# Re-tiling v with six SBUF-to-SBUF transfers per group of heads instead of a round trip through DRAM

## The chip, the cores and the metric

The kernel runs on one core of one Trainium2 chip. The metric is the device time of one execution in microseconds (us), as the median of several runs. A profile is one execution taken by the hardware profiler; its times are counted from the first instruction, and its span ends with the last one.

## What is computed

```python
# q, k, v: (4, 8, 768, 64); sort_net: (4, 8, 8, 8); w_in: (512, 2048); w_out: (2048, 512)
for _ in range(5):
    P = exp(P - max(P)); P = P / (sum(P, -1) + 1e-09); P = P / (sum(P, -2) + 1e-09)
k_sorted = einsum('bhij,bhjcd->bhicd', P, k_b)      # 8 blocks of 96 rows are mixed by P
v_sorted = einsum('bhij,bhjcd->bhicd', P, v_b)
attn = softmax(scale * q_b @ k_sb^T)                # within each block of 96 rows
x = (attn @ v_sb), heads side by side: (3072, 512)
out = relu(x @ w_in)**2 @ w_out
```

An attention in blocks of 96 rows, whose k and v blocks are first mixed by a small matrix, is followed by a feed-forward layer over 3072 rows. All matrix products are made in bf16.

## The kernel before

The work has two streams. The feed-forward stream (`ffn_unit`) takes the 3072 rows in eight units of 384 rows, two to a batch. Each unit makes 64 "hp" matmuls (line 997: x times w_in, 16 tiles of 4), a ReLU on ScalarE and a square on VectorE per tile (lines 1005, 1008), and 48 "op" matmuls (line 1027: times w_out; line 1055 for the last tile), whose results ScalarE copies to `ob` and SyncE sends out. The attention stream works by batch and by pairs of heads (hp 0 to 3); its stages are named by letters. For batches 1 to 3 they are:

- V and N (`s_nat`, line 769): v or k of a group of four heads is mixed by `w_t` on TensorE and cast from PSUM into `vn` or `kn` by ScalarE and VectorE (helper lines 248, 250). A group has two head pairs and uses both PSUM slots of the attention stream (`p2_0`, `p2_1`).
- Z (`s_turn`): two DMA transposes on SyncE, `kx<-kn` (line 824) and `qz<-qi` (line 851), and the copy `kvT<-kx` on VectorE (line 829).
- S (`s_sc`, line 684): the scores, and the exponentials `et` on ScalarE (line 713).
- A (`s_av`, line 875): `et` times the re-tiled v `vblk`, then the reciprocal and the product `ao` on VectorE (lines 885, 886).
- X (`s_xt`, line 910): the DMA transpose `xT<-ao` that feeds the feed-forward units.

Between V and A the v of a group must change its layout: in `vn` a partition holds rows of all eight blocks, in `vblk` a partition is one of the 96 rows of a block. Before, SyncE issues a write `v_way<-vn` to DRAM (line 793, 396 KB), waits for its landing, and issues a read `vblk<-v_way` (line 799). There are two `vn` and three `vblk` buffers, handed out in turn.

The order on every engine is the work of a planner (`Plan.run`) while the program is built. TensorE has two queues of operations, attention and feed-forward. The attention queue is sorted by the due times in `DUES`, one number for each stage and head pair, counted in feed-forward pieces; the planner takes the head of the attention queue when its due time has come and its inputs are ready by the planner's own costs, and else the next feed-forward piece. The other engines take whatever is ready first by those costs. "SP" is SyncE's queue; "WAY" is the time a transfer spends on its way. The chip then runs each engine's list strictly in order, and waits by semaphore.

Of the kernel before, what the change touches and what calls it, by code (L numbers as in the profile page):

```python
# [9 lines left out]
BF16 = mybir.dt.bfloat16  # L10
# [8 lines left out]


DUES = {
    (0, "K"): (-265.0, -237.0, -495.0, -419.0),
    (0, "S"): (-232.5, -234.0, -349.0, -310.0),
    (0, "T"): (-184.0, -236.0, -400.0, -291.5),
    (0, "A"): (-135.0, -150.0, -300.0, -111.0),
    (0, "X"): (-58.0, -109.0, -251.5, -80.5),
    (0, "W"): (-267.0,),
    (1, "V"): (-117.0, -62.5),
    (1, "Q"): (-58.5,),
    (1, "N"): (None, -31.0),  # L30
    (1, "Z"): (None, None, 2.5, 48.5),
    (1, "S"): (-45.5, -5.0, 5.0, 50.0),
    (1, "A"): (-27.0, -4.5, 31.5, 51.5),
    (1, "X"): (40.0, 23.5, 37.0, 53.5),
    (2, "L"): (40.0,),
    (2, "N"): (75.5, 79.0),
    (2, "V"): (60.5, 82.5),
    (2, "Z"): (81.0, 82.5, 94.0, 83.5),
    (2, "S"): (86.0, 86.5, 96.0, 93.5),
    (2, "A"): (86.0, 88.0, 99.0, 94.5),  # L40
    (2, "X"): (97.5, 103.0, 103.0, 102.0),
    (3, "L"): (109.0,),
    (3, "N"): (111.5, 130.0),
    (3, "V"): (112.5, 144.0),
    (3, "Z"): (128.5, 139.0, 153.0, 149.0),
    (3, "S"): (144.0, 153.0, 158.0, 153.5),
    (3, "A"): (145.0, 153.5, 159.5, 154.5),
    (3, "X"): (150.5, 170.0, 236.5, 211.5),
}


# [133 lines left out]
def kernel(  # L185
# [10 lines left out]
    nc = tc.nc  # L196

    B, H, S, D = q.shape
    NB = sort_net.shape[-1]
    BLK = S // NB  # L200
    NH = B * H
    NA = S // 128
    C0 = 128 // NB
    HP = H // 2
# [25 lines left out]
    plan = Plan()  # L230
    rvn, rvb = Ring(2), Ring(3)
# [5 lines left out]
    def cost_f(n):  # L237
        return (0.17 + 0.82e-3 * n, 0.15 + 1.04e-3 * n)
# [7 lines left out]
    def copy(eng, out, in_):  # L246
        if eng == "ACT":
            nc.scalar.copy(out=out, in_=in_)  # L248
        else:
            nc.vector.tensor_copy(out=out, in_=in_)  # L250
# [41 lines left out]
    vn_r, vb_r = [], []  # L292
# [3 lines left out]
        vn_r.append(vn)  # L296
    for n in range(3):
        vb_r.append(const.tile([96, NB, HP, 66], BF16, name=f"vblk{n}"))
    v_way = nc.dram_tensor("v_way", (B, 2, NA, 128, HP * 66), BF16, kind="Internal").ap()

    kn_r = [const.tile([128, NA, 2, D], BF16, name=f"kn{n}") for n in range(4)]
    qi_r = [const.tile([128, NA, 2, D], BF16, name=f"qi{n}") for n in range(4)]
# [150 lines left out]
    for it in range(5):  # L453
        step = plan.add("ACT", 0.26, lambda e: nc.scalar.activation(
            out=p_sb, in_=p_sb, func=AF.Exp), [step])
# [297 lines left out]
    def s_nat(b, g, t, due):  # L753

        if t == 2:
            m, oldm = rvn.take()
        evs = []
        for hp in (2 * g, 2 * g + 1):
            slot, old = r2.take()
            if t == 1:  # L760
                m, oldm = rkn.take()

            def mm(e, hp=hp, slot=slot):
                src = qkv[b][t].rearrange("p (g h) x -> p g (h x)", h=HP)
                w = w_t[:, HP // 2 * b + g, :, :].rearrange("p c i -> p (c i)")
                for h in range(2):
                    r = slice(32 * (2 * (hp % 2) + h), 32 * (2 * (hp % 2) + h + 1))
                    for c in range(4):
                        nc.tensor.matmul(  # L769
                            out=p2[slot][32 * c:32 * (c + 1), h, 0:NA * D],  # L770
                            lhsT=w[r, :],
                            rhs=src[r, g, NA * D * c:NA * D * (c + 1)],
                            start=True, stop=True, tile_position=(r.start, 32 * c))

            def ev(e, hp=hp, slot=slot, m=m):
                dst = (vn_r[m][:, :, 2 * (hp % 2):2 * (hp % 2) + 2, 0:D] if t == 2
                       else kn_r[m])
                copy(e, dst, p2[slot][:, :, 0:NA * D].rearrange("p e (a d) -> p a e d", d=D))

            pe = plan.add("PE", 0.15, mm, [landed[b, t, HP * g, 0], built["t"]] + old, due,  # L780
                          mode="tile")
            readers[b].append(pe)
            op = plan.add(AD, cost_f(2 * NA * D), ev, [pe] + oldm)
            r2.use(slot, pe, op)
            evs.append(op)
            if t == 1:
                rkn.use(m, op)
                k_nat[b, hp] = m, op
        if t == 1:
            return  # L790

        def write(e):
            nc.sync.dma_start(out=v_way[b, g].rearrange("a p x -> p a x"),
                              in_=vn_r[m].rearrange("p a h x -> p a (h x)"))

        w, oldw = rvb.take()

        def read(e):
            nc.sync.dma_start(
                out=vb_r[w].rearrange("p i h x -> p (i h x)"),  # L800
                in_=v_way[b, g].rearrange("a (c i) x -> (a c) (i x)", i=NB))

        wr = plan.add("SP", 0.5, write, evs + ([loaded(b)] if b > 1 else []))
        there = plan.add("WAY", 9.7 if b == 1 and g == 0 else 3.2, lambda e: None, [wr], tail=0.8)
        rd = plan.add("SP", 0.5, read, [there] + oldw)
        back = plan.add("WAY", 3.5, lambda e: None, [rd], tail=0.7)
        rvn.use(m, *evs, there)
        rvb.use(w, back)
        v_blk[b, g] = w, back

    def loaded(b):
        return landed[b, 0, HP, 0]
# [258 lines left out]
    for k in range(2):  # L1071
# [3 lines left out]
        if k == 0:  # L1075
# [3 lines left out]
            out=pt[:, NQ * k:NQ * (k + 1), :], in_=tiles["pt_ps", NQ * k]), [pes[k]]))  # L1079
# [7 lines left out]
    for name in FIRST.split():  # L1087
# [21 lines left out]
        else:  # L1109
# [8 lines left out]
              "A": lambda b, hp, due: s_av(units[b, hp], due),  # L1118
              "X": lambda b, hp, due: s_xt(units[b, hp], due),
              "V": lambda b, g, due: s_nat(b, g, 2, due),  # L1120
              "N": lambda b, g, due: s_nat(b, g, 1, due)}

    def sort_first(b, hp, due):
# [81 lines left out]
```

## Time and profile before

| what | us |
|---|---|
| time, median of 3 runs | 218.34 (217.59 to 218.5) |
| span of the profiled execution | 216.2 |
| TensorE matmul busy | 209.8 (97% of the span) |
| VectorE, ScalarE, GpSimd busy | 109.2, 122.1, 28.3 |
| mean granted TensorE clock | 1.000 |

No time of the profiled execution is given beside its span; the median of the runs lies 2.1 us above that span, which is start and end outside of the first and last instruction. "PE" is TensorE, "DVE" VectorE, "ACT" ScalarE, "POOL" GpSimd, "SPq" SyncE's queue, whose rows are DMA issues and not transfers. Matmuls are pipelined, so a row of the timeline that holds a group of them ends about 0.16 us after the next group has begun. Some matmul records are missing: a group of 12 can be shown as x11.

### The profile page before, as it was taken

The numbers are of one execution on the slowest core, as the hardware profiler recorded it, in microseconds if no ns is written. First come the engines' busy times: TensorE is split into PE (matmuls) and PEld (weight loads), VectorE is DVE, ScalarE is ACT, GpSimd is POOL, SyncE is SP. The second block draws the span as 40 slices with busy tenths as digits, with TensorE's granted clock in tenths as the row PEclk, the third lists the DMA queues.
The fourth block names the chain that finished last, engine by engine and source line by source line (L and its number), as shares of the span: only waits on it lengthen the run. The fifth ranks groups of instructions, "written<-read, shape, count | busy, mean of one in ns | idle before, by whom it ended". The sixth has DMA issues, their size and how long they took to land.

```text
span 216.2 us, 5062 instructions
## 1 busy us (share of the span) xinstructions
PE 209.8 (97%) x2020; PEld 115.9 (54%) x2036; DVE 109.2 (51%) x297; ACT 122.1 (56%) x251; POOL 28.3 (13%) x53
## 2 busy tenths in 40 slices
PE   8998999999999999999999999999999999999994
PEld 2566675446654565445655455445655465455542
DVE  5777677146795446345875047407775154015300
ACT  4876985248765277347774178318874375137421
POOL 7896230000000700000000420000000000000000
PEclk9999999999999999999999999999999999999999
DMA  6999999999978599199995699497978410120012
GB/s 152 212 203 207 207 207 209 193 226 272 176 164 113 84 238 211 25 192 210 179 186 125 105 201 213 87 207 171 170 204 111 102 47 3 49 97 0 0 52 97
DMA packets 47864, 31.92 MB, mean 148 GB/s; under 512 B 27296, under 2 KB 42912, under 8 KB 47840
## 3 DMA queue, kind: packets, MB, share of 16 engines
q1 hardware_dynamic: 35616, 18.35, 40.1%
q0 software_dynamic: 12224, 13.24, 36.9%
q8 instruction: 16, 0.26, 0.5%
q14 instruction: 8, 0.07, 0.1%
HBM read 29.70 MB, written 8.72 MB: 178 GB/s over the span
## 4 chain that ended last, share of the span: by engine, by line
PE 93%; DVE 2%; ACT 2%; issue 1%; DVEq 0%
PE hp L997 37%; PE op L1027 36%; PE p L875 4%; PE p L440 4%; PE p L684 3%; PE p L769 2%; PE op L1055 2%; PE qtp L563 2%; DVE ao L886 1%; PE vbp L733 1%; PE p L649 1%; DVE h L1008 1%; ACT h L1005 1%; PE xtp L928 1%; PE hp L955 0%
## 5 line engine op out<-in xcount | busy, mean ns | idle before, releaser
L997 PE MATMUL hp<-xT,w_in_bf 128*128 128x384 bf16 x506 | 87.6, 326 | 0.0
L1027 PE MATMUL op<-w_out_bf,h 128*128 128x512 bf16 x352 | 83.3, 379 | 0.9 <-issue 0.2
L1008 DVE TENSOR_TENSOR h<-h 128x384 bf16<-128x384 bf16 x128 | 43.9, 355 | 56.2 <-ACT h L1005 55.7
L1005 ACT ACTIVATE h<-hp 128x384 bf16<-128x384 f32 x128 | 61.7, 495 | 17.7 <-PE hp L997 14.9
L997 PEld LDWEIGHTS <-w_in_bf 128*128 128x128 bf16 x506 | 47.7, 98 | 32.2 <-issue 1.1
L1027 PEld LDWEIGHTS <-h 128*128 128x128 bf16 x368 | 33.9, 98 | 37.9 <-issue 1.0
L248 ACT COPY ob<-op 128x512 f32<-128x512 f32 (+2 forms) x25 | 14.2, 568 | 49.1 <-PE op L1027 46.6
L713 ACT ACTIVATE et<-p 96x384 bf16<-96x384 f32 x48 | 19.9, 488 | 6.4 <-PE p L684 6.4
L886 DVE TENSOR_TENSOR ao<-p,rec 96x512 bf16<-96x512 f32 x32 | 22.0, 686 | 1.1
L875 PEld LDWEIGHTS <-et 96*128 96x128 bf16 x256 | 11.2, 97 | 5.5 <-issue 0.7
L885 DVE RECIPROCAL rec<-p 96x8 f32<-96x8 f32 x32 | 6.4, 201 | 11.1 <-PE p L875 10.5
L1144 POOL COPY held<-xT 1x3 bf16<-1x3 bf16 (+1 forms) x2 | 0.4, 183 | 85.0 <-DMA xT<-ao 85.0
L440 PE MATMUL p<-ones 128*128 128x512 bf16 (+1 forms) x28 | 9.2, 460 | 1.1 <-DVE ones L274 1.1
L875 PE MATMUL p<-vblk,et 96*128 96x65 bf16 x192 | 9.4, 193 | 0.1
L250 DVE CAST vn<-p 128x768 bf16<-128x768 f32 x6 | 5.7, 958 | 7.3 <-PE p L769 7.2
L250 DVE CAST kn<-p 128x768 bf16<-128x768 f32 x5 | 4.8, 958 | 9.1 <-PE p L769 9.1
L684 PEld LDWEIGHTS <-kvT 64*128 64x128 bf16 x256 | 6.2, 94 | 5.5 <-issue 3.6
L829 DVE COPY kvT<-kx 128x768 bf16<-128x768 bf16 x10 | 8.5, 850 | 0.0
L248 ACT CAST vn<-p 128x768 bf16<-128x768 f32 x6 | 4.8, 798 | 5.8 <-PE p L769 5.8
L324 POOL DMA_DIRECT2D kb<-in_k_dram x10 | 6.5, 648 | 4.1 <-DMA w_in_bf<-in_moe_w_in_dram 2.0
L248 ACT CAST kn<-p 128x768 bf16<-128x768 f32 x5 | 4.0, 806 | 4.7 <-PE p L769 4.7
L324 POOL DMA_DIRECT2D vb<-in_v_dram x10 | 6.3, 633 | 2.3 <-DMA w_in_bf<-in_moe_w_in_dram 2.1
(81 smaller groups left out, 118.8 us busy)
## 6 DMA issues: line engine op xcount, KB each, us to landing
out_dram<-ob SPq DMA_DIRECT2D x23, 256.0 KB, 3.4
v_way<-vn SPq DMA_DIRECT2D x6, 396.0 KB, 5.1
vblk<-v_way SPq DMA_DIRECT2D x6, 396.0 KB, 4.3
vb<-in_v_dram POOLq DMA_DIRECT2D x6, 384.0 KB, 11.7
kb<-in_k_dram POOLq DMA_DIRECT2D x6, 384.0 KB, 10.4
qb<-in_q_dram POOLq DMA_DIRECT2D x6, 384.0 KB, 13.1
w_in_bf<-in_moe_w_in_dram POOLq DMA_DIRECT2D x4, 512.0 KB, 10.4
w_out_bf<-in_moe_w_out_dram POOLq DMA_DIRECT2D x4, 512.0 KB, 15.7
```

What stands on the lines that cost most here:

```text
L248: nc.scalar.copy(out=out, in_=in_)
L250: nc.vector.tensor_copy(out=out, in_=in_)
L324: nc.gpsimd.dma_start(out=dst, in_=src)
L440: nc.tensor.matmul(out=p2[slot][:, 0, 0:128 * r].rearrange("p (r x) -> p r x", r=r), lhsT=ones, rhs=ones[:, None, :].to_broadcast([128, r, ...
L684: nc.tensor.matmul(out=scp[:, h, BLK * n:BLK * (n + 1)], lhsT=u.ksT[64 * h:64 * (h + 1), HS * hf + BLK * n:HS * hf + BLK * n + 128], rhs=( ...
L713: nc.scalar.activation(out=et[:, h, 0:HS].rearrange("p (n c a) -> p n c a", c=C0, a=NA), in_=st["p"][0:96, h, 0:HS].rearrange("p (n a c) - ...
L875: nc.tensor.matmul(out=oup[:, h, 66 * n:66 * n + D + 1], lhsT=et_r[u.et[hf]][:, h, BLK * n:BLK * n + 128], rhs=(u.vs[:, NQ * hf + n, h, 0: ...
L886: nc.vector.tensor_tensor(out=u.ao[:, n0:n0 + NQ, :, :].rearrange("p n e d -> p e n d"), in0=ov[:, :, :, 0:D], in1=rec[:, :, :, None].to_b ...
L997: nc.tensor.matmul(out=t["hp", nt][:, 0:HS], lhsT=w_in_bf[:, kc, 128 * nt:128 * (nt + 1)], rhs=xT[:, kc, t0:t0 + HS], start=(kc == 0), sto ...
L1005: nc.scalar.activation(out=t["h1", nt], in_=t["hp", nt][:, 0:HS], func=AF.Relu)
L1008: nc.vector.tensor_tensor(out=t["h2"][:, nt, :], in0=t["h1", nt], in1=t["h1", nt], op=ALU.mult)
L1027: nc.tensor.matmul(out=t["op", mt], lhsT=t["h2"][:, nt, 128 * mt:128 * (mt + 1)], rhs=w_out_bf[:, nt, :], start=(nt == 0), stop=(nt == NT ...
```

## The change

It does two things. `s_nat` no longer writes v of a group to `v_way` and reads it back. It issues six DMAs on SyncE, one for each sixth `a` of the 96 rows: each takes the 128 partitions of `vn[:, a]` (264 bf16 elements each) and lays them into 16 partitions of `vblk`, eight blocks side by side. The six are a chain in the planner (each counts as ready after the one before), at a planned 0.4 us each; after the last the planner counts 9.7 and 6.5 us on the way for batch 1 and 2.4 us for batches 2 and 3. The `vn` buffer is held until the moves have landed, and the `vblk` buffer must be free before the first move. The second thing: all due times are set anew.

```diff
-    (2, "N"): (75.5, 79.0),
-    (2, "V"): (60.5, 82.5),
+    (2, "N"): (58.0, 58.0),
+    (2, "V"): (78.5, 62.5),
...
-    v_way = nc.dram_tensor("v_way", (B, 2, NA, 128, HP * 66), BF16, kind="Internal").ap()
...
-        def write(e):
-            nc.sync.dma_start(out=v_way[b, g].rearrange("a p x -> p a x"),
-                              in_=vn_r[m].rearrange("p a h x -> p a (h x)"))
+        def move(e, a):
+            nc.sync.dma_start(out=vb_r[w][C0 * a:C0 * (a + 1)].rearrange("c i h x -> c i (h x)"),
+                              in_=vn_r[m][:, a].rearrange("p h x -> p (h x)"))
 
         w, oldw = rvb.take()
-
-        def read(e):
-            nc.sync.dma_start(
-                out=vb_r[w].rearrange("p i h x -> p (i h x)"),
-                in_=v_way[b, g].rearrange("a (c i) x -> (a c) (i x)", i=NB))
-
-        wr = plan.add("SP", 0.5, write, evs + ([loaded(b)] if b > 1 else []))
-        there = plan.add("WAY", 9.7 if b == 1 and g == 0 else 3.2, lambda e: None, [wr], tail=0.8)
-        rd = plan.add("SP", 0.5, read, [there] + oldw)
-        back = plan.add("WAY", 3.5, lambda e: None, [rd], tail=0.7)
-        rvn.use(m, *evs, there)
+        ops = evs + ([loaded(b)] if b > 1 else []) + oldw
+        for a in range(NA):
+            mv = plan.add("SP", 0.4, lambda e, a=a: move(e, a), ops)
+            ops = [mv]
+        back = plan.add("WAY", (9.7, 6.5)[g] if b == 1 else 2.4, lambda e: None, [mv], tail=1.4)
+        rvn.use(m, *evs, back)
         rvb.use(w, back)
         v_blk[b, g] = w, back
```

The new order shows best on SyncE. For batch 2, before, its list from the first output of the unit on reads as follows (`qz2` belongs to the first head pair, `qz0`, `qz1`, `qz2` to the next three; the names after "waits" are semaphores, of which DMAHW0 to DMAHW7 tell of landed DMAs).

```order
L976 DMA out_0_dram<-ob_1743 128x512 [waits DMAHW7_49,Activation_49]
L793 DMA v_way<-vn0_104 128x6x264 [waits DMAHW0_49,DVE_49]
L824 DMA_TRANSPOSE kx2_121<-kn2_113 128x6x128 [waits DMAHW1_49]
L851 DMA_TRANSPOSE qz2_102<-qi2_117 128x6x128 [waits DMAHW2_49,DVE_49,PE_49]
L824 DMA_TRANSPOSE kx0_119<-kn3_114 128x6x128 [waits DMAHW3_49,DVE_49]
L799 DMA vblk2_110<-v_way 96x2112 [waits DMAHW4_49,DMAHW0_49]
L793 DMA v_way<-vn1_106 128x6x264 [waits DMAHW5_49,DVE_49,Activation_49]
L851 DMA_TRANSPOSE qz0_92<-qi3_118 128x6x128 [waits DMAHW6_49]
L824 DMA_TRANSPOSE kx1_120<-kn1_112 128x6x128 [waits DMAHW7_49]
```

The same place now, from the first move on; the six moves of the two groups are shuffled into each other.

```order
L792 DMA vblk2_110<-vn0_104 16x8x264 [waits DMAHW0_49,DVE_49,Activation_49]
L818 DMA_TRANSPOSE kx2_121<-kn2_113 128x6x128 [waits DMAHW1_49]
L792 DMA vblk2_110<-vn0_104 16x8x264 [waits DMAHW2_49]
L792 DMA vblk0_108<-vn1_106 16x8x264 [waits DMAHW3_49,DVE_49,Activation_49]
L792 DMA vblk2_110<-vn0_104 16x8x264 [waits DMAHW4_49]
L792 DMA vblk0_108<-vn1_106 16x8x264 [waits DMAHW5_49]
L792 DMA vblk2_110<-vn0_104 16x8x264 [waits DMAHW6_49]
L792 DMA vblk0_108<-vn1_106 16x8x264 [waits DMAHW7_49]
L792 DMA vblk2_110<-vn0_104 16x8x264 [waits DMAHW0_49]
L792 DMA vblk0_108<-vn1_106 16x8x264 [waits DMAHW1_49]
L792 DMA vblk2_110<-vn0_104 16x8x264 [waits DMAHW2_49]
L792 DMA vblk0_108<-vn1_106 16x8x264 [waits DMAHW3_49]
```

Behind these twelve rows stand `qz2<-qi2`, the last move, and the six transposes of the other three head pairs. The query transpose of the first head pair, second behind the write before, now stands behind eleven moves and one transpose. Each DMA waits on the semaphore of the eighth DMA ahead of it, which the names DMAHW0 to DMAHW7 in turn show.

For batch 3 the list of SyncE now begins so, behind two outputs (before, behind one). `qz0` is of the first head pair, `qz1` of the second.

```order
L970 DMA out_0_dram<-ob_2397 128x512 [waits DMAHW5_49,Activation_49]
L970 DMA out_0_dram<-ob_2435 128x512 [waits DMAHW6_49,Activation_49]
L792 DMA vblk1_109<-vn0_104 16x8x264 [waits DMAHW7_49,DVE_49]
L818 DMA_TRANSPOSE kx0_119<-kn2_113 128x6x128 [waits DMAHW0_49]
L792 DMA vblk1_109<-vn0_104 16x8x264 [waits DMAHW1_49]
L845 DMA_TRANSPOSE qz0_92<-qi2_117 128x6x128 [waits DMAHW2_49,DVE_49]
L792 DMA vblk1_109<-vn0_104 16x8x264 [waits DMAHW3_49]
L818 DMA_TRANSPOSE kx1_120<-kn3_114 128x6x128 [waits DMAHW4_49,DVE_49]
L792 DMA vblk1_109<-vn0_104 16x8x264 [waits DMAHW5_49]
L792 DMA vblk2_110<-vn1_106 16x8x264 [waits DMAHW6_49,DVE_49,Activation_49]
L792 DMA vblk1_109<-vn0_104 16x8x264 [waits DMAHW7_49]
L792 DMA vblk2_110<-vn1_106 16x8x264 [waits DMAHW0_49]
```

The moves of the first group now alternate with the transposes of the first two head pairs; before, one write stood ahead of them. On TensorE the same matmuls stand in another order: its list is the same up to the second piece of the first feed-forward unit, and again from the last attention group of batch 3 to the end.

More of the change, by code (lines that the diff above doesn't have):

```diff
@@ L21 @@
 DUES = {
[L22 to L35, printed above, removed]
-    (2, "N"): (75.5, 79.0),
-    (2, "V"): (60.5, 82.5),
[L38 to L48, printed above, removed]
+    (0, "K"): (-252.5, -268.0, -363.0, -361.5),
+    (0, "S"): (-224.5, -216.5, -336.0, -308.0),
+    (0, "T"): (-192.5, -234.0, -358.0, -287.0),
+    (0, "A"): (-157.5, -200.0, -286.0, -129.5),
+    (0, "X"): (-68.5, -134.0, -285.0, -106.0),
+    (0, "W"): (-275.0,),
+    (1, "V"): (-131.0, -82.5),
+    (1, "Q"): (-69.0,),
+    (1, "N"): (None, -40.5),
+    (1, "Z"): (None, None, -15.5, 9.5),
+    (1, "S"): (-44.5, -23.0, -14.0, 49.0),
+    (1, "A"): (-35.5, -16.5, 9.5, 51.0),
+    (1, "X"): (-32.5, 50.5, 40.5, 55.5),
+    (2, "L"): (56.0,),
+    (2, "N"): (58.0, 58.0),
+    (2, "V"): (78.5, 62.5),
+    (2, "Z"): (80.0, 81.0, 93.0, 85.5),
+    (2, "S"): (81.5, 87.5, 94.5, 93.5),
+    (2, "A"): (85.5, 91.0, 103.0, 95.0),
+    (2, "X"): (98.0, 94.0, 106.0, 98.5),
+    (3, "L"): (110.5,),
+    (3, "N"): (135.0, 139.5),
+    (3, "V"): (127.5, 140.5),
+    (3, "Z"): (137.5, 144.5, 156.5, 145.5),
+    (3, "S"): (143.0, 149.0, 161.0, 152.0),
+    (3, "A"): (149.0, 157.5, 161.0, 153.0),
+    (3, "X"): (155.5, 187.5, 266.5, 203.0),
 }
```

## Prediction

> **What bounds the kernel now.** I read the page's first part, then the waits of TensorE, then the timelines of TensorE and of SyncE's queue in batches 2 and 3.
>
> ```profile
> span 216.2 us, 5062 instructions
> PE 209.8 (97%) x2020; PEld 115.9 (54%) x2036; DVE 109.2 (51%) x297; ACT 122.1 (56%) x251; POOL 28.3 (13%) x53
> ```
>
> TensorE's share of 97% alone would not say that it works at its pace, since overlapping matmuls count as busy. The waits of TensorE do:
>
> ```profile
> PE p L440 <- DVE ones L274: 1.1, 1, 1.1
> PE p L875 <- ACT qz L248: 0.5, 1, 0.5
> PE p L684 <- DVE ao L886: 0.3, 1, 0.3
> PE op L1027 <- issue: 0.2, 1, 0.2
> ```
>
> The first three lie in the first 20 us, where the order of the work is not changed; the fourth stands beside a missing record (the row at 93.33 below has 11 of 12 matmuls). No wait for `vblk` or `v_way` is among them. So the round trip through DRAM is hidden entirely, and removing it frees nothing by itself.
>
> How close is TensorE to its own pace? The undisturbed units at the end give the pace:
>
> ```profile
> 171.28 10.56 PE L997 MATMUL hp<-xT,w_in_bf 128*128 128x384 bf16 x64
> 181.68 10.52 PE L1027 MATMUL op<-w_out_bf,h 128*128 128x512 bf16 x47
> 192.04 10.56 PE L997 MATMUL hp<-xT,w_in_bf 128*128 128x384 bf16 x64
> ```
>
> From start to start, 64 hp matmuls take 10.40 us (0.1625 each), and 48 op matmuls, one unrecorded, 10.36 us (0.216 each). I laid every group of the program end to end at the pace that its kind has in the timeline (a switch into or out of the S groups costs about 0.1 us, and counts). From 20 us to the last matmul group the timeline is 0.96 us longer than this sum. **That 0.96 us is all that a better order can win.**
>
> **The change part by part.** *TensorE's work.* The matmuls are the same. I counted the groups in both orders: the S groups are entered from another line 22 times before and 22 times after, the V and N groups 11 and 11 times. Since only such switches cost extra, the end-to-end sum is the same: 0.
>
> *DRAM traffic.* Six writes and six reads of 396 KB go; six times six moves come that carry what the writes carried. Less load on the DMA queues: a gain only where one is late, and by the waits none is: 0.
>
> *SyncE's queue.* Here the change adds: 36 issues for 12. For batch 2 before:
>
> ```profile
> 91.34 0.39 SPq L793 DMA_DIRECT2D v_way<-vn  x1
> 91.78 1.69 SPq L824 DMA_TRANSPOSE kx<-kn  x1
> 93.57 1.31 SPq L851 DMA_TRANSPOSE qz<-qi  x1
> 94.97 2.12 SPq L824 DMA_TRANSPOSE kx<-kn  x1
> 97.19 0.53 SPq L799 DMA_DIRECT2D vblk<-v_way  x1
> 97.82 0.37 SPq L793 DMA_DIRECT2D v_way<-vn  x1
> 98.25 1.94 SPq L851 DMA_TRANSPOSE qz<-qi  x1
> ...
> 104.70 1.24 SPq L851 DMA_TRANSPOSE qz<-qi  x1
> 106.04 0.52 SPq L799 DMA_DIRECT2D vblk<-v_way  x1
> ```
>
> The queue issues without a pause from 91.34 on: it is the busiest place that the change touches. A write occupies it 0.37 to 0.39 us and the next follows 0.05 later; a read takes 0.53 and 0.10. A move is not in the trace: I bound it by these, 0.42 to 0.60, and take 0.45, since its source side is the write's. A transpose costs 1.24 to 2.12; I take 1.32 with its gap, the undisturbed value. How long they are then on the way, the DMA view gives as medians:
>
> ```profile
> v_way<-vn SPq DMA_DIRECT2D x6, 396.0 KB, 5.1
> kx<-kn SPq DMA_TRANSPOSE x10, 3.9
> qz<-qi SPq DMA_TRANSPOSE x10, 3.6
> out_dram<-ob SPq DMA_DIRECT2D x1, 64.0 KB, 1.6
> DMA to landing us min/median/max: 2.8/4.0/6.1
> ```
>
> (The last line is the view of `qz` in batch 2.) A move of 66 KB lands between 1.6 and 5.1 us after its issue; I take 2.5, nearer to the output of its size.
>
> *Batch 2.* TensorE's rows around the first S, and a cast and a copy of the same stretch:
>
> ```profile
> 93.33 2.54 PE L1027 MATMUL op<-w_out_bf,h 128*128 128x512 bf16 x11 [0.16 <-issue]
> 95.80 0.38 PE L769 MATMUL p<-vb,w_t 32*32 32x384 bf16 x16
> 96.11 1.90 PE L1027 MATMUL op<-w_out_bf,h 128*128 128x512 bf16 x8
> 97.84 1.46 PE L997 MATMUL hp<-xT,w_in_bf 128*128 128x384 bf16 x8
> 99.24 0.51 PE L684 MATMUL p<-qz,kvT 64*128 64x96 bf16 x16
> 103.08 0.66 PE L875 MATMUL p<-vblk,et 96*128 96x65 bf16 x16
> 96.32 0.96 DVE L250 CAST vn<-p 128x768 bf16<-128x768 f32 x1 [1.78 <-PE p L769]
> 98.05 0.59 ACT L248 COPY ob<-op 128x512 f32<-128x512 f32 x1 [1.02 <-PE op L1027]
> ```
>
> In the new order 28 hp matmuls of that unit stand ahead of the first S, not 8: 20 x 0.1625 = 3.25 us later; one S group of batch 1 that is no longer cut in two gives back 0.24. So S comes due at 99.24 + 3.01 = 102.25. Its query: ahead of the first V group now stand 20 op matmuls and one group (0.4) fewer than ahead of the V at 95.80, so it starts at 95.80 - 4.32 - 0.4 - 0.24 = 90.8. Its cast on VectorE ends 1.48 after the start (95.80 to 97.28 in the rows), so the first move goes at 92.35. Then one move, one transpose and ten more moves: 92.35 + 0.45 + 1.32 + 4.5 = 98.6 for the issue of `qz2`, and with 3.6 on the way it lands at 102.2. **It comes just in time, where before, issued at 93.57 and with 4.0 on the way, it was 1.7 us ahead of need.** With 0.42 a move and 2.8 on the way it is 1.1 early; with 0.60 and 6.1, 4.1 late. Since the ends are not alike, I charge 0.3. The next: the last move of the second group goes at 98.6 + 1.32 = 99.95 and lands at 102.5; A needs it at 103.08 + 0.92 = 104.0. The last query stands behind one more move and five transposes: issued at 99.95 + 0.45 + 6.6 = 107.0, landed at 110.6; its S, by the end-to-end sum, is due at 112.1. So the first wait decides, and those behind it have more room.
>
> *Batch 3.* Before, the first S:
>
> ```profile
> 139.66 0.38 SPq L793 DMA_DIRECT2D v_way<-vn  x1
> 142.19 1.22 SPq L851 DMA_TRANSPOSE qz<-qi  x1
> 150.16 0.51 PE L684 MATMUL p<-qz,kvT 64*128 64x96 bf16 x16
> ```
>
> Now two outputs stand ahead of the first move. The second belongs to an op tile that ends, by the end-to-end sum, at about 141.6; its copy takes 0.59 and the issue 0.4, so the first move goes at 142.6 and not at 139.66: the queue stands behind a copy of ScalarE for 2.9 us. `qz0` follows two moves and a transpose: 142.6 + 0.9 + 1.32 = 144.8, landed at 148.4. S has 8 hp matmuls fewer ahead of it, and the 0.24 from batch 1: due at 150.16 - 1.30 - 0.24 = 148.6. The second query is issued seven moves and two transposes (`qz0` itself and `kx1`) later: 144.8 + 2.64 + 3.15 = 150.6, landed at 154.2, due by the same sum at 154.35; the third at 157.7 against 158.0. Three that come 0.15 to 0.3 ahead of need, where before the first query had five microseconds. A wait at one shifts those behind it, so they don't add. I charge 0.3, with 0 and 2.5 as ends.
>
> *Batch 1.* The first write, its way to landing (the longest of the view of `v_way`), and the first A:
>
> ```profile
> 43.30 0.37 SPq L793 DMA_DIRECT2D v_way<-vn  x1
> DMA to landing us min/median/max: 3.8/4.3/10.0
> 59.26 0.66 PE L875 MATMUL p<-vblk,et 96*128 96x65 bf16 x16
> ```
>
> The write landed at 53.3, behind the loads of the batch. The moves share their queue with two outputs, as the write did; I let the last of the first group land by 55. A is due 12 hp matmuls earlier than at 59.26, at 57.3. Cost 0, cover 2.3 us.
>
> *V and N closer together.* Two V or N groups that share both PSUM slots now follow each other at 1.28 us twice; the casts free the second slot at 1.48 (above). About 0.1 us each: 0.2.
>
> *What goes.* In batch 2 the second read, issued at 106.04, landed 6.2 later, at 112.3, just as A began:
>
> ```profile
> DMA to landing us min/median/max: 6.2/6.2/6.2
> 112.43 0.41 PE L875 MATMUL p<-vblk,et 96*128 96x65 bf16 x8
> ```
>
> Such places the new order does not have. Of the 0.96 us I let 0.4 go (0 to 0.96).
>
> Sum: 0.3 + 0.3 + 0.2 − 0.4 = +0.4. On the span of 216.2 that gives 216.6, and with the 2.1 us between the profile's span and the median of the runs, **218.7 us**.
>
> **Rivals.** *The queue becomes the bound (slower).* If a move costs SyncE 0.60 like a read, and a transpose behind them 2.12 like the one at 94.97, the query of batch 2 is issued at 92.35 + 0.6 + 2.12 + 6 = 101.1 and lands at 104.7: 2.4 us late. For batch 3, nine moves stand ahead of the second query: 9 x 0.15 + 0.8 = 2.15 later than above, 2.0 late. 218.34 + 2.4 + 2.0 − 0.2 (the other terms) = 222.5. It decides from about 0.55 us a move. For it: the queue has no pause as it is, and each DMA waits for the eighth ahead of it, so landings over 3.6 us slow the issues. Against: the rows of 0.37.
>
> *The moves themselves are slow (slower).* A write of 128 partitions lands 3.8 us after its issue when nothing is ahead of it, the 64 KB output 1.6:
>
> ```profile
> DMA to landing us min/median/max: 3.8/3.8/3.8
> ```
>
> So 396 KB take 2.2 us of transfer, 0.37 for a sixth. If a move into 16 partitions takes twice that, 0.75, eleven moves fall 11 x 0.3 = 3.3 us behind their issue, and S of batch 2 waits 3.2 us; in batch 3 the transposes between give time, about 0.5. Time 218.34 + 3.7 = 222.0. The Trainium skill, "SBUF — State Buffer", section "Door 1: The DMA port swizzle", speaks against the change here: partitions 0 to 15 reach 4 of 16 ports, measured there at 104 GB/s. By that, an estimate from the page, a move takes 0.65 us, and the time would be about 221. No row of this trace has such a transfer, so I can't say that it agrees; moves that follow each other go to other partitions, which may hide it.
>
> *The waits vanish (faster).* If the moves land early, all of the 0.96 us may go and nothing come: 217.4 at best. For it: the DRAM reads are gone from the queue. Against: the new order ties S to its query more closely.
>
> *The change does not do what it says:* the order shows the moves and no `v_way`, so no chance is given to that.
>
> **How the numbers follow.** My forecast, waits of a few tenths in place of others, 217.8 to 219.4: 0.66. Queue-bound: 0.16. Slow moves: 0.09. Faster: 0.09. A measurement of this kernel can tell about 0.5%, 1.1 us. Under 217.25 lies little, since the floor forbids more: 0.04, by scatter of the runs. Over 219.4 lie the two slower cases and a little of the forecast's end: 0.26. Same: 0.70. The range leaves out 0.1 at each side: from 217.4, the floor, to 220.9, which takes in the milder half of the slower cases.
>
> **What would show it.** Right: PE waits after 20 us stay under 1.5 us in all; moves issue at 0.4 to 0.5 us; the first S of batches 2 and 3 starts within 0.5 us of 102.3 and 148.7. The forecast is wrong if SPq rows of moves are over 0.55 us, if `qz` lands more than 4.5 us after its issue in batch 2, or if PE waits for `qz`, `kvT` or `vblk` for over a microsecond. It would be wrong on the other side if the span falls under 215.1.

## The result and the profile after

| kernel | us, median (range) | ratio to before, 95% interval |
|---|---|---|
| before | 218.34 (217.59 to 218.53) | |
| changed | 225.15 (224.89 to 226.19) | 1.034 (1.032 to 1.036) |
| changed, measured again later on another occasion (e13) | 223.50 (222.71 to 223.99) | 1.026 (1.024 to 1.028) |

The changed kernel is 5.6 to 6.8 us slower, outside the range that was forecast. The profiled execution is one of 224.89 us with a span of 223.1 us and a mean granted clock of 0.992, where before had 216.2 and 1.000. (Single runs of e2, e3 and e9, and of before beside e13 and e14, were over 1.5% longer than the fastest of their kernel; the ratios leave them out.)

The waits of TensorE in the changed kernel, largest first (total, times, longest):

```profile
PE p L683 <- DMA qz<-qi: 4.6, 2, 2.4
PE p L439 <- DVE ones L274: 1.1, 1, 1.1
PE p L869 <- ACT qz L248: 0.5, 1, 0.5
PE p L683 <- DVE ao L880: 0.3, 1, 0.3
```

The last three were there before. The first line is new: two S groups wait for their query transposes. In the chain that ended last, SyncE's queue now has a share, and the moves' line has most of it:

```profile
PE 86%; SPq 6%; DMA 3%; DVE 1%; ACT 1%; issue 1%; ACTq 0%
```

SyncE's queue in batch 2 (start, time that the issues take, line, operation, how many):

```profile
91.03 0.33 SPq L970 DMA_DIRECT2D out_dram<-ob  x1
92.72 0.58 SPq L792 DMA_DIRECT2D vblk<-vn  x1
93.35 2.38 SPq L818 DMA_TRANSPOSE kx<-kn  x1
95.77 6.38 SPq L792 DMA_DIRECT2D vblk<-vn  x10
102.20 1.31 SPq L845 DMA_TRANSPOSE qz<-qi  x1
...
146.58 0.33 SPq L970 DMA_DIRECT2D out_dram<-ob  x1
147.00 0.59 SPq L792 DMA_DIRECT2D vblk<-vn  x1
...
152.93 3.81 SPq L792 DMA_DIRECT2D vblk<-vn  x6
156.78 1.29 SPq L845 DMA_TRANSPOSE qz<-qi  x1
```

(The last four rows are from the same view in batch 3.) Ten moves hold the queue from 95.77 to 102.20, 0.64 us each with the gap. In the DMA view the moves' way to landing is short, and the transposes land sooner than before, when the medians were 3.9 and 3.6:

```profile
vblk<-vn SPq DMA_DIRECT2D x36, 66.0 KB, 2.7
kx<-kn SPq DMA_TRANSPOSE x10, 2.8
qz<-qi SPq DMA_TRANSPOSE x10, 2.8
```

So the transfers are quick and the issues are slow. TensorE at the same place:

```profile
98.18 4.71 PE L991 MATMUL hp<-xT,w_in_bf 128*128 128x384 bf16 x28
105.08 0.52 PE L683 MATMUL p<-qz,kvT 64*128 64x96 bf16 x16 [2.19 <-DMA qz<-qi]
105.53 2.49 PE L991 MATMUL hp<-xT,w_in_bf 128*128 128x384 bf16 x8
120.72 7.07 PE L1021 MATMUL op<-w_out_bf,h 128*128 128x512 bf16 x32
161.29 0.52 PE L683 MATMUL p<-qz,kvT 64*128 64x96 bf16 x16 [2.37 <-DMA qz<-qi]
```

From start to start the 28 hp matmuls would hand over at 98.18 + 28 x 0.1625 = 102.7; S starts at 105.08, 2.35 us later (the view counts 2.19 of it as idle, since the last matmul's row ends 0.16 after the hand-over). The second S of batch 3, at 161.29, comes 2.53 us late by the same count. The row behind the first S is the second surprise: eight hp matmuls in 2.49 us, 0.31 each, where the row above has 0.168. The granted clock by stretches of 3.41 us (busy us of TensorE and its count; the number behind POOL's is the clock):

```profile
102.42:105.83 3.41, 1.22 (x21) 0.76 (x20) 0.81 (x3) 1.21 (x3) 0.00 (x0) 1.00 0.59 125
105.83:109.24 3.41, 3.41 (x20) 1.83 (x18) 1.48 (x3) 2.13 (x6) 0.00 (x0) 0.50 0.78 151
109.24:112.66 3.42, 3.42 (x47) 2.04 (x46) 2.85 (x8) 2.37 (x7) 0.00 (x0) 1.00 0.77 149
```

The stretch that holds the wait is followed by one of 3.41 us at half clock. The second wait, in batch 3 (up to 161.29), had no such sequel here.

### The profile page after: what moved, and what is told of

Its sections match the earlier page's. It is cut to its first block, busy times and chain, and to the rows that moved or that the text cites. A ratio compares the mean times of both kernels' runs of the same rounds, so it can differ in the third digit from the quotient of the medians.

```text
span 223.1 us, 5107 instructions
## 1 busy us (share of the span) xinstructions
PE 213.4 (96%) x2036; PEld 116.9 (52%) x2036; DVE 109.9 (49%) x297; ACT 123.0 (55%) x251; POOL 28.4 (13%) x53
## 4 chain that ended last, share of the span: by engine, by line
PE 86%; SPq 6%; DMA 3%; DVE 1%; ACT 1%; issue 1%; ACTq 0%
PE op L1021 34%; PE hp L991 33%; SPq L792 5%; PE p L439 4%; PE p L869 4%; PE p L683 3%; DMA qz<-qi 3%; PE p L768 2%; PE op L1049 2%; PE qtp L562 1%; SPq L818 1%; PE vbp L732 1%; PE p L648 1%; PE xtp L922 1%; PE hp L949 0%
## 5 line engine op out<-in xcount | busy, mean ns | idle before, releaser
L991 PE MATMUL hp<-xT,w_in_bf 128*128 128x384 bf16 x506 | 89.4, 330 | 0.0
L1021 PE MATMUL op<-w_out_bf,h 128*128 128x512 bf16 x368 | 85.0, 379 | 0.0
L1002 DVE TENSOR_TENSOR h<-h 128x384 bf16<-128x384 bf16 x128 | 44.4, 356 | 51.9 <-ACT h L999 51.6
L869 PEld LDWEIGHTS <-et 96*128 96x128 bf16 x256 | 11.7, 99 | 5.5 <-issue 1.3
L683 PE MATMUL p<-qz,kvT 64*128 64x96 bf16 x160 | 5.8, 204 | 4.6 <-DMA qz<-qi 4.6
```

What stands on the lines that cost most here:

```text
L683: nc.tensor.matmul(out=scp[:, h, BLK * n:BLK * (n + 1)], lhsT=u.ksT[64 * h:64 * (h + 1), HS * hf + BLK * n:HS * hf + BLK * n + 128], rhs=( ...
L869: nc.tensor.matmul(out=oup[:, h, 66 * n:66 * n + D + 1], lhsT=et_r[u.et[hf]][:, h, BLK * n:BLK * n + 128], rhs=(u.vs[:, NQ * hf + n, h, 0: ...
L991: nc.tensor.matmul(out=t["hp", nt][:, 0:HS], lhsT=w_in_bf[:, kc, 128 * nt:128 * (nt + 1)], rhs=xT[:, kc, t0:t0 + HS], start=(kc == 0), sto ...
L1002: nc.vector.tensor_tensor(out=t["h2"][:, nt, :], in0=t["h1", nt], in1=t["h1", nt], op=ALU.mult)
L1021: nc.tensor.matmul(out=t["op", mt], lhsT=t["h2"][:, nt, 128 * mt:128 * (mt + 1)], rhs=w_out_bf[:, nt, :], start=(nt == 0), stop=(nt == NT ...
```

## The experiments

The theory after the result: SyncE needs 0.64 us for each move, moves stand ahead of the queries, so S waits; the rest of the loss is the lower clock. Rivals: the new due times lose by themselves; the moves' bytes are the load; the planner's wrong cost is the fault; the clock costs little.

**e1: due times of before, moves on SyncE.** `DUES` of before in the changed kernel.

> The six moves stay on SyncE, the due times are those of before. Theory (SyncE is overbooked just ahead of the first query in batch 2 and the second in batch 3, 0.64 us a move): in this order only two moves stand ahead of the first query of batch 2, so no wait of TensorE over 0.7 us there or in batch 3, no loss of clock, 218 to 219.5 us. Rival A (moves into 16 partitions are slow on their way, wherever they stand): TensorE waits for vblk, 222 or more. Rival B (the new order of TensorE costs by itself): 218.3.

Measured 220.12 us (219.73 to 220.53), ratio 1.011 (1.009 to 1.012). That is above both the theory's range and rival B. TensorE waits for a query once, 0.9 us up to 110.85: this query was issued at 106.02, behind eleven of the batch's moves, and took 4.7 us to land. A wait of 0.4 us for `xT` is new too; where the rest of the 2 us goes is not located. The planner made an order of its own here (on TensorE it differs from the one of before from about 60 us on), so the run doesn't isolate the moves.

**e2: new due times, round trip through DRAM.** `DUES` of the changed kernel in the kernel before.

> The round trip through DRAM as before, with the new due times; the planner makes its own order from them. Theory (the due times were set for a plan with moves at 0.4 us, and fit no other): the last A of batch 3 stands right ahead of the first hp matmul that needs its xT, 3 to 4.5 us of wait there and 1 to 2 us at the same place of batch 2; no wait for a query; 222 to 225 us. Rival A (the moves are the whole loss): 218 to 219. Rival B (the new due times are the whole loss): 225.

Measured 229.46 us (227.94 to 231.43), ratio 1.050 (1.045 to 1.055): worse than every expectation, and the worst of the four combinations. TensorE's waits there are of another kind:

```profile
PE hp L997 <- DMA xT<-ao: 5.8, 3, 2.9
```

The first feed-forward matmuls of later units wait for their input: with V as late as these due times put it and two trips of 3.2 and 3.5 us in the plan, A and X presumably come too late. That the due times are no good with the DRAM trip doesn't say that they are bad with the moves.

**e3: the same plan, the moves issued by GpSimd.** `nc.sync` becomes `nc.gpsimd` in `move`; TensorE's order is untouched.

> The changed kernel with one word altered: the moves are issued by GpSimd, while the planner still books them on SyncE, so the list of TensorE is the same to the row. Theory: SyncE holds only the transposes, the query of batch 2 lands before 99, the waits of 2.35 and 2.5 us and the lost clock are gone: 217.7 to 219.3 us. Rival A (moves into 16 partitions are slow themselves): A waits for vblk, 222 or more. Rival B (the new order of TensorE costs by itself): 225.

Measured 221.50 to 228.81 us in four runs, ratio 1.023 (1.016 to 1.029), above the theory's range. As the theory had it, no S waits for a query; instead A waits for v:

```profile
PE p L869 <- DMA vblk<-vn: 3.4, 1, 3.4
```

The view of `vblk` in batch 2 of this run has the reason:

```profile
DMA to landing us min/median/max: 4.8/6.2/7.2
```

A move issued by GpSimd takes it 0.53 us, but lands 4.8 to 7.2 us later, where SyncE's land after 2.5 to 3.0. The wait has only moved.

**e4: the planner told the truth.** `plan.add("SP", 0.4, ...)` becomes `0.64`.

> The changed kernel with the planner's cost of a move at the measured 0.64 us in place of 0.4; due times as in the change. Theory: the planner now puts the first S of batch 2 at 107 and fills the time with feed-forward work, so the wait for that query goes; but the attention ends later than the feed-forward work can cover, and the first hp matmul of batch 3 waits 4 to 5.5 us for xT: 221 to 224.5 us. Rival B (the order of TensorE by itself): no statement. If the planner's cost alone were at fault: 218.5.

Measured 227.61 us (226.55 to 228.23), ratio 1.044 (1.041 to 1.048): slower still, and 3 us above the expected range. No S waits for a query any more, but the first hp matmuls of the next units wait:

```profile
PE hp L991 <- DMA xT<-ao: 5.1, 3, 3.2
```

The planner now puts S, A and X later, and the two feed-forward units of a batch are used up before the next batch's `xT` is there. So a wrong cost in the plan is not the fault; with these due times, moves at their real price do not fit either way.

**e5: half of the moves left out.**

```diff
         def move(e, a):
+            if b > 1 and a % 2:
+                return
```

> The changed kernel with every second move of batches 2 and 3 left out (three of six per group; the other halves of vblk keep old values, so the result is not computed), the order of TensorE unchanged. Theory (the moves' 0.64 us each on SyncE's queue make the queries late): in batch 2 five of eleven moves ahead of the first query go, 3.2 us, so the query lands at about 101.9, before 102.57 when S is due; the wait of 2.35 us goes, and with it the half-clock stretch of 3.41 us, worth 1.7. In batch 3 four or five of nine go, 2.6 to 3.2 us, and the wait of 2.53 goes. Time 225.15 - 2.35 - 1.7 - 2.5 = 218.6 (218.0 to 219.8), mean clock 0.998 or more. Rival (the new order of TensorE itself loses, whatever SyncE does): over 222, waits of qz at the same two places.

Measured 218.57 us (218.05 to 219.05), ratio 1.002 (1.000 to 1.004), clock 0.999 to 1.000 in all ten runs. Both waits are gone. In SyncE's queue five moves are left where ten stood:

```profile
93.50 2.49 SPq L822 DMA_TRANSPOSE kx<-kn  x1
96.09 3.11 SPq L796 DMA_DIRECT2D vblk<-vn  x5
99.25 1.29 SPq L849 DMA_TRANSPOSE qz<-qi  x1
```

The query is issued 2.95 us earlier, and all but 0.4 us of the loss is gone. This is the run that decides against the due times as the cause: the groups of matmuls stand on TensorE in the order of the changed kernel, and that order costs 0.4 us (0.9 at most, by the interval). TensorE's rows at the places shown above:

```profile
98.24 4.71 PE L995 MATMUL hp<-xT,w_in_bf 128*128 128x384 bf16 x28
102.89 0.52 PE L683 MATMUL p<-qz,kvT 64*128 64x96 bf16 x16
116.87 7.07 PE L1025 MATMUL op<-w_out_bf,h 128*128 128x512 bf16 x32
155.01 0.52 PE L683 MATMUL p<-qz,kvT 64*128 64x96 bf16 x16
```

Set against them, the changed kernel loses 2.25 us from the hp matmuls of 98.18 to the first S, 1.66 from there to the 32 op matmuls, where the half clock lies, and 2.43 from there to the second S of batch 3. That is 6.3 of the 6.4 us by which its span is longer (223.1 against 216.7).

**e7: moves in batch 1 alone.** Due times of before; batches 2 and 3 keep the round trip.

> Due times of before; moves on SyncE in batch 1 only, the round trip through DRAM in batches 2 and 3. Theory (a move costs only where SyncE's queue is full, and in batch 1 it is not): 217.6 to 218.9, no wait of TensorE over 0.5 us after 20 us. Rival (moves cost wherever they are, or the planner's other order costs): 219.3 to 220.5, as with moves in all batches.

Measured 217.94 us (217.48 to 218.75), ratio 0.999 (0.996 to 1.001). Twelve moves where SyncE has room cost nothing, and win nothing.

**e8: what an issue costs.** Twelve DMAs of six forms near the end, when SyncE is idle.

> The changed kernel and, near its end where SyncE is idle, twelve extra DMAs on SyncE, two of each form: (a) a move, 128x264 to 16x8x264; (b) 128x264 to 128x264 in SBUF; (c) 128x264 to DRAM; (d) 16x2112 from DRAM; (e) 16x2112 to 16x2112 in SBUF; (f) half a move, 64x264 to 8x8x264. They carry nothing that is used. Theory A (an issue costs more when it ends in SBUF, whatever the shape): a, b, d, e, f 0.50 to 0.62 us, c 0.33 to 0.40. Theory B (the split of a row of partitions into 16x8 costs): a and f 0.55 to 0.62, b 0.37, c 0.37, d and e 0.37 to 0.52. Theory C (cost by the number of rows): a and b 0.60, f 0.45 to 0.50, d and e under 0.45. Time as of the changed kernel, 224.5 to 226.5, since SyncE waits there for outputs.

SyncE's rows (two issues of each form, the total behind the start):

```profile
191.67 0.33 SPq L970 DMA_DIRECT2D out_dram<-ob  x1
192.06 1.22 SPq L1067 DMA_DIRECT2D vblk<-vn  x2
193.32 1.24 SPq L1069 DMA_DIRECT2D vn<-vn  x2
194.61 1.06 SPq L1071 DMA_DIRECT2D way<-vn  x2
197.06 0.79 SPq L1073 DMA_DIRECT2D vblk<-way  x2
197.90 1.23 SPq L1075 DMA_DIRECT2D vblk<-vblk  x2
199.23 1.45 SPq L1077 DMA_DIRECT2D vblk<-vn  x2
```

The row of two spans the gap between them. The three whole forms with both ends in SBUF take 0.58 to 0.60 us an issue, with the split into 16x8 or without, and half a move 0.66 to 0.75. With one end in DRAM it is 0.33 to 0.36 (`vblk<-way`) and 0.59 and 0.43 (`way<-vn`). None of the three theories holds: not the destination (`vblk<-way` ends in SBUF and is cheap), not the split, not the number of rows. In these rows a DMA within SBUF is the dear one, but for the first `way<-vn`, which stands right behind such DMAs and took as much; with two issues of each form, why is open.

The one run took 223.47 us, below what was expected, and TensorE had the same two waits as the changed kernel (4.4 us), but kept its clock:

```profile
101.68:105.09 3.41, 1.43 (x9) 0.74 (x8) 1.44 (x4) 1.48 (x4) 0.00 (x0) 1.00 0.56 123
105.09:108.50 3.41, 3.30 (x47) 2.31 (x47) 1.30 (x3) 2.82 (x7) 0.00 (x0) 1.00 0.71 141
```

**e9: issues without bytes.** In place of each move left out in e5, SyncE issues a DMA of one partition and 528 bytes within SBUF.

> As the run with half the moves, but in the place of each move left out SyncE issues a DMA of one partition and 528 bytes from the same vn to a scratch row in SBUF (result not computed). Theory (it is the time that SyncE spends on an issue, about 0.6 us whatever the size, as the issue probe has it): the time comes back, 224 to 226.5, with waits for qz at the first S of batch 2 and the second of batch 3. Rival (it is the bytes or the transfers of the moves, which the half version also halved): 218 to 219.5, no wait for qz.

Measured 229.48 us (227.34 to 231.09), ratio 1.048 (1.044 to 1.052): the loss is back, and more than was expected, since a tiny DMA holds the queue longer than a whole move (the profile is of the run of 231.09 us):

```profile
95.70 0.88 SPq L795 DMA_DIRECT2D tiny<-vn  x1
96.71 1.25 SPq L800 DMA_DIRECT2D vblk<-vn  x2
98.06 1.59 SPq L795 DMA_DIRECT2D tiny<-vn  x2
...
102.75 0.63 SPq L800 DMA_DIRECT2D vblk<-vn  x1
103.42 1.29 SPq L853 DMA_TRANSPOSE qz<-qi  x1
```

The first query is issued at 103.42, 1.2 us later than in the changed kernel, and TensorE waits 7.2 us for queries in all. Bytes are not the cause; the time of the issues is, whatever they carry.

**e10: SyncE's list in order of need.** The order is changed after planning, for SyncE alone: six moves of batch 2 go behind its last query, those of the second group of batch 3 behind its second query.

> All moves on SyncE, planned as in the changed kernel, TensorE's order unchanged; only SyncE's list is put in order of need: in batch 2 the six moves of vblk2, which A reads last, go behind the last query, in batch 3 those of the second group behind the second query. Theory (the queries are late because moves that nobody needs yet stand ahead of them): the first query of batch 2 is issued at about 98.3 and lands at 101.2, before 102.57; the last move lands at about 114.8, just when A needs it; in batch 3 the second query lands 1.9 us earlier, so of the 2.5 us wait at most 0.6 stays. Time 218.4 to 220. Rival (SyncE's 18 us of issues for batch 2 are too many in any order): TensorE waits 1 to 3 us for vblk or qz later in the batch, 221 to 225.

Measured 221.95 us (221.47 to 224.19), ratio 1.019 (1.015 to 1.023): between the two expectations. No S waits for a query, but:

```profile
PE p L683 <- DVE rec L881: 1.8, 1, 1.8
...
PE p L871 <- DMA vblk<-vn: 0.9, 1, 0.9
```

The last moves of batch 2 land 3.5 to 4.1 us after their issue and A waits 0.9 us. In batch 3 a k transpose now stands behind four moves; VectorE's copy `kvT<-kx` starts at 159.46, after 2.46 us of waiting for it, and `rec` and `ao` of two finished A groups stand behind it on VectorE, so their PSUM slots come free late and S waits 1.8 us. This order wins about half of the loss back; with all moves on SyncE the other half stays.

**e11: the moves shared out.** Every second move of batches 2 and 3 is issued by GpSimd.

> The changed kernel with every second move of batches 2 and 3 issued by GpSimd instead of SyncE, TensorE's order unchanged. Theory (SyncE's queue is the cause; with half its moves gone it is in time, as with half the moves left out): 218.3 to 219.8, no wait over 0.5 us after 20 us. Rival (GpSimd's moves land 5 to 7 us after their issue and slow the transposes beside them): TensorE waits 1 to 3 us for vblk in batch 2, 220 to 224, and more where that empties a clock window.

Measured 220.28 us (220.22 to 220.82), ratio 1.010 (1.008 to 1.012). One wait for a query is left, 1.7 us in batch 2, since transposes beside GpSimd's moves land 4.8 to 6.1 us after their issue. The time lies above the theory's range: that wait is the loss that is left. It is the fastest of the complete versions with these due times.

**e6: moves on GpSimd, due times of before.**

> Due times of before, the moves issued by GpSimd and planned there at 0.6 us. Theory (only SyncE's queue was short; GpSimd has 0.53 us a move to spare): no wait of TensorE for qz or vblk over 0.5 us, 217.4 to 218.9, that is within 0.5% of before, or below 217.3 if SyncE's emptier queue wins more. Rival (moves issued by GpSimd land 4.8 to 7.2 us after their issue, and transposes beside them 5 to 9, as in the run before with moves on GpSimd): TensorE waits for vblk or xT by 1 to 3 us in batch 2 or 3, 219.5 to 222, and single runs with a half-clock window are 2 to 2.5 us longer.

Measured 220.47 us (219.11 to 221.83), ratio 1.011 (1.008 to 1.014): in the rival's range, not the theory's. Its profile, of the run of 219.11 us, shows only waits up to 0.5 us; where the other runs lose their time stays open.

**e12, e13, e14: what the clock costs.** Fillers are matmuls of ones put ahead of the S group that waits:

```diff
+                if (u.b, u.hp, hf) == (2, 0, u.halves[0]):
+                    fill(2.2, slot)
```

> The changed kernel with nine more matmuls of ones (0.216 us each, 1.9 us in all, into a PSUM slot that the scores overwrite) ahead of the first S of batch 2, where TensorE waits 2.35 us for its query; every other row of every engine is the same. They compute nothing. Theory (a wait that empties more than about 2 of the clock's 3.41 us leaves TensorE at half clock for the next 3.41 us): the wait is filled, the clock stays full, and the time falls by half of 3.41, 1.7 us, to 223.5 (223.0 to 224.2), mean clock 0.998 or more in nearly all runs. Rival (the half clock is not due to the idle time, or costs nothing that counts): 225, mean clock 0.992. If the fillers delay the scores: 225.5 to 227.

Measured 224.91 us (223.91 to 225.44), ratio 1.032 (1.029 to 1.036). The fillers do what they should; the hp matmuls behind S keep 0.163 us:

```profile
102.76 2.10 PE L439 MATMUL p<-ones 128*128 128x512 bf16 x9
105.00 0.52 PE L685 MATMUL p<-qz,kvT 64*128 64x96 bf16 x16
105.45 1.47 PE L993 MATMUL hp<-xT,w_in_bf 128*128 128x384 bf16 x8
...
112.69 0.34 PE L685 MATMUL p<-qz,kvT 64*128 64x96 bf16 x8 [0.67 <-DVE rec L881]
```

Mean clock 1.000 in three of four runs. But the time fell by 0.2 us in the median and 1.0 in the profiled pair (223.91 against 224.89), not by 1.7: part of what TensorE gains it waits for VectorE at 112.69. The 0.2 says little, since the changed kernel itself differs by 1.65 us between two occasions. To settle the size, it was run again, beside one with fillers in both batches.

> The changed kernel itself, unaltered, beside the next kernel on the same chip. Both theories: 224.5 to 226.2, mean clock 0.985 to 0.992 in most runs. If some runs keep a clock of 0.998 or more, theory (half a clock window costs 1.7 us) has these 1.2 to 1.7 us shorter, rival (the lost clock costs little, since TensorE then waits elsewhere) less than 0.6.

> As the run with fillers ahead of the first S of batch 2, and nine more such matmuls ahead of the second S of batch 3. Theory (lost clock costs 1.7 us wherever a wait empties a window): mean clock 0.999 in all runs, 223.3 to 224.2. Rival (the clock costs little): clock full, but 224.5 to 225.3, within 0.3 us of the changed kernel in the same rounds.

e13, unaltered, gave 222.71, 223.20 and 223.50 at a clock of 1.000, and 223.87 and 223.99 at 0.992 and 0.990. In its profile the second wait, not the first, took the clock down: with only 1.10 us busy from 155.29 to 158.70. e14 kept 0.999 to 1.000 in all six runs and took 223.47 us (222.83 to 224.97), ratio 1.027 (1.024 to 1.031): no faster than e13, with a wait of 0.5 us for VectorE in its profile. There the fillers of batch 3 also cost time themselves: they hold the second S until 159.46, while its query, issued at 155.43, landed 3.3 us later, at 158.7.

The rows settle more than the medians, since the groups of matmuls stand in the same order in all these runs. From the first S of batch 2 to the 32 op matmuls, TensorE takes 13.98 us in e5. The changed kernel with its half clock takes 1.66 more, about the 1.7 that I worked out. Where the clock was kept, though, the same stretch takes 0.07 more in e13, 0.37 in e8 and 0.82 in e12. So keeping the clock is worth 0.8 to 1.6 us here, because part of it goes into waits elsewhere; between single runs of e13 it is 0.4 to 1.3. The two theories each hold in part.

## Why the prediction was wrong

**The step that failed** is the price of a move: "I bound it by these, 0.42 to 0.60, and take 0.45, since its source side is the write's." It was 0.60 with the gap's 0.04 on top, beyond the far end of the bounds. The source alone doesn't set it: the two rows compared have one end in DRAM (0.37 to 0.39 and 0.53 us), and in e8 a DMA with both ends in SBUF is dearer than either. With eleven moves ahead of the first query, this is 11 x 0.19 = 2.1 us. The k transpose among them held the queue 2.38 us where 1.28 was taken, another 1.1; the first move came 0.4 later than reckoned. Together 98.6 becomes 102.20, and the query lands at 105.04 after only 2.84 us on the way, where S was due at 102.7. The due time of S itself was nearly right (102.25 forecast). Why the k transpose took so long is open; it overlaps a fetch of instructions on the DMA engines that starts at 93.44, and the four other transposes after 60 us that held the queue over 1.45 us stand beside such fetches too (64.59, 112.15, 159.17, 172.06), but no run tests that.

**Batch 3** failed by the same step and one more. Its first move was reckoned right, 4.4 us later like everything behind the first wait (147.00 against 142.6). The second query came 1.8 us behind the reckoning, then took 4.5 us to land where its neighbours took 2.8:

```profile
DMA to landing us min/median/max: 4.5/4.5/4.5
```

(The view of `qz` from 156 to 158 us.) With 2.8 it would have come only 0.8 us late. The other 1.7 us came with two instruction fetches on the DMA engines at 159.2 and 159.4; in e8 and e13 this landing took 4.4 as well. That they cause it is only a guess.

**The order of TensorE** was judged right: it has little cost of its own, as e5 shows (0.4 us over before). That e5's 218.57 us are close to the forecast of 218.7 is luck, since the forecast's +0.4 was made of two waits for queries and a gain of 0.4, and e5 has no such wait. Batch 1 was right too (no wait; e7).

**Small slips in the working.** The read with its gap is 0.53 + 0.10 = 0.63 us and not 0.60, which is nearly what a move cost. Two groups that follow at 1.28 us, where the casts free the slot at 1.48, lose 0.2 us each by these numbers, not 0.1; in the trace it is 0.22 each (at 92.45 and 149.73), about what e5 keeps. The query of batch 2 landed 4.3 us after its issue before, not 4.0. And of the 2.1 us between span and median only 1.8 lies between a run's time and its own span (224.89 and 223.1); the rest is scatter.

**The rival** "the queue becomes the bound" had the right mechanism, and its waits, 2.4 + 2.0 us, came as 2.35 and 2.53; its time of 222.5 us was still too low, for want of the clock. It was given 0.16, because the write of 0.37 us was taken as the move's kin and the read of 0.53 not. The rival of slow transfers falls: moves land after 2.5 to 3.0 us in batch 2. The Trainium skill, "SBUF — State Buffer", section "Door 1: The DMA port swizzle", would, by the estimate made from it in the prediction, have a move into 16 partitions take 0.65 us of transfer. In e8 a move lands 2.5 to 2.6 us after its issue and a copy from 16 partitions to 16 after 2.3, so no run separates an effect of the ports; e9 shows that it doesn't make this loss.

**Not foreseen** was the clock. No step asked what a wait does to the matmuls behind it. Of the 6.3 us that the rows of the changed kernel lose against e5, 4.7 are the two waits and 1.66 is the half clock. In e13's profile, of a run 6.0 us over before (223.87), the waits are 1.65 and 2.38 us and a half clock in batch 3 takes 1.6, which is 5.6 of it. Its runs that kept the clock have no profile, so what they lose by is open.

## What to carry over

Price a DMA by its own form, or take the dear end of the bounds when it will stand in a queue without pauses: eleven times a small error made 2.1 of the 3.6 us by which the first query was issued late. Six small transfers in place of one make the issuing engine the resource, and the one behind them pays. The Trainium skill, "DMA: Bandwidth & Descriptors", section "🎯 Rules for kernel authors", says to coalesce many small transfers into one, and that under 64 KB one pays mostly overhead. The traces agree even just above that size: six moves of 66 KB hold SyncE 3.8 us, a write and a read 0.9. Moving issues to another engine (e11) or into another order (e10) helped only in part: it works as far as the sum of issues and landings fits between the first V and the last S.

## What the runs showed of the hardware

- **Issues.** In e8 a DMA within SBUF holds SyncE 0.58 to 0.60 us whether it moves 66 KB in 128 rows or in 16, and 0.66 to 0.75 for 33 KB; in e9 it is 0.75 to 0.88 for 528 bytes. From DRAM into 16 partitions it is 0.33 to 0.36 (e8). The moves of the changed kernel took 0.55 to 0.61 us in batches 2 and 3, and up to 0.99 in batch 1.
- **The clock.** In the traces the clock of TensorE changes only at multiples of 3.413 us after its first rise, and stretches at half clock between the matmuls last 3.413 us (105.83 to 109.24 here) or 6.827 (e2, e9). A window at full clock with 1.27 us or less of busy time was followed by half clock (0.35 in e4, 0.75 in e2, 0.84 and 1.27 in e9, 1.10 in e13, 1.22 here), one with 1.43 or more was not (1.43 and 1.47 in e8; 1.59 and 1.86 in e3). So a wait of 2.2 us inside one window loses the clock, and one of 2.4 us across two does not, by chance of where it falls. The Trainium skill, "TensorE: Matmul & The Clock Gate", section "🔬 Part 1: The HAM clock gate (the "warmup" mystery)", has such a free-running window of 3413 ns, and the traces agree; it lets the clock fall after an idle window, and here a window that was a third busy was enough.
- **GpSimd's moves.** The same move issued by GpSimd lands 4.8 to 7.2 us after its issue in batch 2 of e3, 3.1 to 6.4 in e11 and 2.8 to 5.0 in e6; by SyncE it lands after 2.5 to 3.0 in batch 2 of the changed kernel.
